# Strided V copies moved to VectorE, one w_out sum moved to GpSimd, and a piece list of its own for chunk 1

## The chip, the cores and the metric

The kernel runs on one core of a Trainium2 chip. The time is the device time of one execution in microseconds (us); several executions of each kernel are measured and their median is taken. A profiled execution gives the trace: what each engine did, when, and what ended its waits. The engines are TensorE (PE, with its weight loads PEld), VectorE (DVE), ScalarE (ACT), GpSimd (POOL) and SyncE (SP, which here only issues DMAs). Each engine works through its own queue in order.

## The reference

```python
def _attn_ref(q, k, v):                      # 8 batches, 8 heads, 576 positions, 64 wide
    ...
    mask_local = (rel >= 0) & (rel < stride)                  # heads 0 to 3, stride 32
    mask_strided = (rel >= 0) & (pos[None, :] % stride == pos[:, None] % stride)   # heads 4 to 7
    ...
    scores = np.where(masks[None, :, :, :], scores, -1000000000.0)
    ...
    return np.matmul(attn, v).astype(np.float32)

def _moe_ref(x, w_in, w_out, alpha):         # 4608 tokens, 512 -> 2048 -> 512
    h = x @ w_in
    g = np.maximum(h, 0.0) + alpha * np.minimum(h, 0.0)
    return (g @ w_out).astype(np.float32)
```

The attention's output, with the heads side by side, is the `x` of the two-layer network. Half of the heads look at the 32 latest positions, the other half at positions that are equal modulo 32.

## The kernel before

**Attention.** Two heads make a pair, four pairs a batch: two local ones, then two strided ones. Pairs are numbered g = 0 to 31, so batch 2 is pairs 8 to 11. The work on a pair is cut into pieces that are put into one list: T and Tk transpose q and k of two pairs (`transpose_piece`); S computes the scores, their exponentials on ACT and a multiplication by the mask on GpSimd (`score_both`, masks on lines 421 and 428); P multiplies with V and divides by the row sums on DVE (`pv_piece`, reciprocal on line 456, multiplication on line 458); X transposes the result into `xT` (`x_piece`), which for most pairs a DMA transposition does in its place. S hands the second half of its exponentials and its mask to a list `defer`, from which each later step takes one entry. PSUM for P, T, X and half of S comes from one pool of three buffers (`ps`).

The strided heads' V is loaded into `stv` (`load_v`, line 169) and copied, 72 partitions by 1024 elements for each half, into `vs`, where each head row has a column of ones beside it (`cast_v`, through `cast_copy`, line 189 on GpSimd and 187 on DVE).

**Network.** The tokens are worked in nine chunks of 512, over a ring `xT` of three batches. Linear 1 has 16 pieces to a chunk (`lin1_piece`): four matmuls into one of three PSUM buffers `hps` (line 627), a ReLU of the negated sum on ACT (line 637), and one DVE instruction that makes `gT` of both (line 639) and frees the buffer. Chunk 0 has a plain linear 2. Chunks 1 to 8 do linear 2 as 2x2 blocks with seven products in place of eight, each product in two pieces of eight matmuls (`fast_piece`, line 696). This needs sums of blocks of `gT` (`g_sums`: four sums, each in a LOW and a HIGH half of 128x1024 elements, written to `sg`) and sums of blocks of `w_out`, made once (`w_sums`: three written to `wt`, the fourth written over a block of `wout16`). All of them are DVE instructions on line 645. Product P6 needs sum 1, P5 sum 0, P7 sum 2, P3 sum 3.

**Order.** It is written out by hand and kept. While chunk n runs (30 pieces: 16 of linear 1, then 14 of linear 2), the attention of batch n+1 is put between its pieces. `acc` spreads the attention pieces evenly, at a lower rate (0.4) in linear 1; chunk 1 has 22 of them, as the list starts up there, the next chunks 17. The sums of `gT` come after the pieces that `SUMS` names. In chunk 1 the two halves of the fourth `w_out` sum come after pieces 2 and 5. Copies, loads and casts of the next batch hang on attention pieces: `cast_v` of batch c on the P pieces of step g = 4c (for batch 2 on the S piece of step 8), the load of the next strided V behind the second copy.

In the list, 22 pieces stand in chunk 1: Tq, Tk for pairs 8 and 9; S8; S9, two P of pair 8; S10, two P of pair 9; S11, P, Tq, P, Tk, P (pair 10, and q and k for pairs 12 and 13); S12 and three P of pair 11; S13, one P of pair 12, X of pair 11. The last one ends the `xT` that chunk 2 needs.

Of the kernel before, what the change touches and what calls it, by code (L numbers as in the profile page):

```python
# [10 lines left out]
F16 = mybir.dt.float16  # L11
ALU = mybir.AluOpType
# [19 lines left out]
def kernel(  # L32
# [10 lines left out]
    nc = tc.nc  # L43
# [7 lines left out]
    FAST = 1  # L51

    LOW, HIGH = slice(0, 4), slice(4, 8)
    SUMS = {10: [(0, LOW)], 16: [(1, LOW)], 17: [(0, HIGH)], 18: [(1, HIGH)],
            20: [(2, LOW)], 21: [(2, HIGH)], 23: [(3, LOW)], 25: [(3, HIGH)]}

# [2 lines left out]
    cpool = ctx.enter_context(tc.tile_pool(name="const", bufs=1))  # L59
    spool = ctx.enter_context(tc.tile_pool(name="stage", bufs=3))  # L60
    tpool = ctx.enter_context(tc.tile_pool(name="tl", bufs=4))
    hpool = ctx.enter_context(tc.tile_pool(name="half", bufs=4))
# [12 lines left out]
            name=nc.get_next_instruction_name(), act_func_set_id=6, ins=[], outs=[]  # L75
# [9 lines left out]

    win16 = cpool.tile([128, 4, 2048], F16)
    wout16 = cpool.tile([128, 16, 512], F16)
    wt = cpool.tile([128, 3, 8, 256], F16)
    xT = cpool.tile([128, 4, RING], F16)

    NE = 6
# [14 lines left out]
    def load_qk(b, strided, nm):  # L106

        h0 = 4 if strided else 0  # L110
        src = q if nm == "q" else k
        if strided and b:
            t16 = hpool.tile([128, 2, 512], F16, tag=f"{nm}s", bufs=3, name=f"{nm}s")
            cast16[(b, True, nm)] = t16
        else:
            t16 = hpool.tile([128, 2, 512], F32, tag=f"{nm}l", bufs=2, name=f"{nm}l")
            loaded[(b, strided, nm)] = t16
        base = src[b, h0 : h0 + 1, 0:1, :]
        eng = nc.sync if (b > 2 and not strided) or (b == 0 and strided) else nc.gpsimd
        keep(eng.dma_start(t16, bass.AP(  # L120
            tensor=base.tensor, offset=base.offset,
            ap=[[8 * D, 64], [2 * S * D, 2], [S * D, 2], [1, 8 * D]])))
# [11 lines left out]
            keep(nc.sync.dma_start_transpose(o, qks[nm].rearrange("p h c -> p (h c)")))  # L134

    def cast_s(b, nm, eng):
        t16 = hpool.tile([128, 2, 512], F16, tag=f"{nm}s", bufs=3, name=f"{nm}s")
        if eng[0] == eng[1]:
            cast_copy(eng[0], t16, loaded[(b, True, nm)])
        else:  # L140
            for f in range(2):
                cast_copy(eng[f], t16[:, f : f + 1, :], loaded[(b, True, nm)][:, f : f + 1, :])
        cast16[(b, True, nm)] = t16
# [47 lines left out]
    def cast_v(b, pr, eng):  # L191

        v16 = vss[b % 2]
        cast_copy(eng, v16[0:72, 2 * pr : 2 * pr + 2, :, 0:64],
                  loaded[b][0:72, 1024 * pr : 1024 * pr + 1024].rearrange(
                      "p (h t d) -> p h t d", h=2, t=8))
        cast16[(b, True, "v")] = v16
# [294 lines left out]
    npair = 4 * B  # L492
# [44 lines left out]
    for g in range(7, npair + 2):  # L537
        c = g // 4
        a, p, t = g, g - 1, g + 1
        okA = 8 <= a < npair  # L540
        okP = 8 <= p < npair
        okT = 8 <= t < npair and (t % 4 == 0 or t < 4 * DX and t % 2 == 0)
        nP = len(pairs[p].pgroups) if okP else 0
        seq = []
        if okA:
            seq.append(("S", lambda a=a: score_both(pairs[a])))
        if okP:
            seq.append(("P", Pv(p, 0)))
        if okT:
            seq.append(("T", T(t // 2, "q")))  # L550
        if 8 <= g - 2 < npair and not pairs[g - 2].xd:
            seq.append(("X", X(g - 2)))
        if okP:
            seq.append(("P", Pv(p, 1)))
        if okT:
            seq.append(("Tk", T(t // 2, "k")))
        if nP == 3:
            seq.append(("P", Pv(p, 2)))
        if not seq:
            seq.append(("N", lambda: None))  # L560

        todo = [(c, pr) for pr in range(2)] if g % 4 == 0 and 8 <= g < npair else []

        if g % 4 == 1 and 9 <= g and c + 1 < B:
            todo = [(c + 1, nm) for nm in "qk"]
        lastP = max([i for i, z in enumerate(seq) if z[0] == "P"], default=len(seq) - 1)
        nslots = [i for i, z in enumerate(seq) if z[0][0] != "S"] or list(range(len(seq)))
        for i, (kind, fn) in enumerate(seq):
            extra = []
            if todo and i in nslots:  # L570
                left = len([z for z in nslots if z >= i])
                cnt = -(-len(todo) // max(1, left))
                extra = [todo.pop(0) for _ in range(min(cnt, len(todo)))]

            def run(fn=fn, extra=extra, g=g, c=c, kind=kind, lastp=(i == lastP), first=(i == 0)):
                fn()
                for b, pr in extra:
                    if pr in ("q", "k"):
                        cast_l(b, pr, "act")
                        if b + 1 < B:  # L580
                            load_qk(b + 1, False, pr)
                        continue
                    cast_v(b, pr, "pool")
                    if pr == 1 and b + 1 < B:
                        load_v(b + 1, True)
                if kind == "Tk" and g % 4 == 3 and c + 3 < B:
                    load_tail(c + 3, False)
                if lastp:
                    if 4 * DX <= g - 1 < npair and pairs[g - 1].xd:
                        x_dma(pairs[g - 1])  # L590
                    if g % 4 == 3 and DX <= c + 1 < B:
                        transpose_d()
                    if g % 4 == 2 and DX <= c and c + 1 < B:
                        load_d(c + 1)
                    if g % 4 == 1 and DX < c and c + 1 < B:
                        load_v(c + 1, False)
                if first and 4 * DX <= g - 3 < npair and pairs[g - 3].xd and pairs[g - 3].strided:
                    x_copy(pairs[g - 3])
            feed(run, g - 2 if kind == "X" else -1)
# [39 lines left out]
        keep(nc.vector.scalar_tensor_tensor(  # L639
            gTs[n][:, m, :], neg, oma[:, m : m + 1], hps, op0=ALU.mult, op1=ALU.add))  # L640

    sums = {}

    def sub(eng, o, x, y, op=ALU.subtract):
        keep(eng.tensor_tensor(o, x, y, op=op))  # L645

    def g_sums(n, k, P):

        if k == 0 and P.start == 0:
            sums["t"] = cpool.tile([128, 4, 8, 256], F16, tag="sg", name="sg")  # L650
        st, g = sums["t"], gTs[n].rearrange("r (p j) t -> r j p t", j=2)
        lo, hi = slice(0, 256), slice(256, 512)
        x, y, op = (
            (g[:, 0, P, hi], g[:, 1, P, hi], ALU.add),
            (st[:, 0, P], g[:, 0, P, lo], ALU.subtract),
            (g[:, 0, P, lo], g[:, 0, P, hi], ALU.subtract),
            (g[:, 1, P, lo], st[:, 1, P], ALU.subtract))[k]
        sub(nc.vector, st[:, k, P], x, y, op)

    def w_sums(k, P):  # L660

        w = wout16.rearrange("r (p j) c -> r j p c", j=2)
        lo, hi = slice(0, 256), slice(256, 512)
        o, x, y, op = (
            (wt[:, 0, P], w[:, 1, P, hi], w[:, 0, P, hi], ALU.subtract),
            (wt[:, 1, P], wt[:, 0, P], w[:, 0, P, lo], ALU.add),
            (wt[:, 2, P], w[:, 1, P, lo], wt[:, 1, P], ALU.subtract),
            (w[:, 0, P, hi], w[:, 0, P, hi], w[:, 0, P, lo], ALU.subtract))[k]
        sub(nc.vector, o, x, y, op)

    PRODUCTS = ("P1", "P4", "P2", "P6", "P5", "P7", "P3")
    cur = {}
# [1 line left out]
    def fast_piece(n, i):  # L674

        name, tb = PRODUCTS[i // 2], i % 2
        last = n == NCH - 1
        g = gTs[n].rearrange("r (p j) t -> r j p t", j=2)
        w = wout16.rearrange("r (p j) c -> r j p c", j=2)
        st = sums["t"]  # L680
# [3 lines left out]
            "P4": ("Z", g[:, 1, :, hi], wt[:, 2]),  # L684
            "P2": ("X", g[:, 1, :, lo], w[:, 1, :, lo]),
            "P6": ("Y", st[:, 1], wt[:, 1]),
            "P5": ("Z", st[:, 0], w[:, 0, :, hi]),
            "P7": ("Y", st[:, 2], wt[:, 0]),
            "P3": ("V", st[:, 3], w[:, 1, :, hi]),
        }[name]  # L690
# [3 lines left out]
        z = cur[bank]  # L694
# [159 lines left out]
    def attn_n(n, end):  # L854
        for _ in range(n):
            attn_step(end)
        if n == 0:
            attn_step(0)
# [30 lines left out]
    for n in range(1, NCH):  # L889
        ab = attn_until(n + 1) if n + 1 < B else len(pieces)  # L890
        left = ab - pos["i"]
        acc = 0.0
        for i in range(30):
            if i < 16:
                lin1_piece(n, i)
                if n == 1 and i in (2, 5):
                    w_sums(3, slice(0, 4) if i == 2 else slice(4, 8))
            else:
                fast_piece(n, i - 16)
            for which, part in SUMS.get(i, ()):  # L900
                g_sums(n, which, part)
            acc += left / (18.4 if n == B - 2 else 19.6) * (0.4 if i < 16 else 1.0)
            cnt = int(acc)
            acc -= cnt
            attn_n(cnt, ab)
        while pos["i"] < ab:
            attn_step(ab)
# [30 lines left out]
```

## Time and profile before

| | us |
|---|---|
| median of three runs | 320.64 |
| lowest, highest | 318.5, 324.51 |
| profiled execution | 317.97 |
| its span, first to last instruction | 316.0 |

| engine | busy us | share of the span |
|---|---|---|
| TensorE | 302.8 | 96% |
| VectorE | 244.2 | 77% |
| ScalarE | 193.0 | 61% |
| GpSimd | 139.0 | 44% |

Linear 1 (line 627) holds 134.2 us of TensorE's busy time. The longest groups on DVE are line 639 (104.5 us, 144 instructions of 743 ns) and the sums of `gT` (60 us in three forms). GpSimd's are the masks (24 on each of two lines, 1.29 and 1.33 us each) and 14 copies of strided V (1.2 us each).

A line of the timeline reads: start, length (both us), engine, line of the program, operation, output<-input, partitions and elements, and in brackets the idle time before it and what ended it. A busy TensorE is not TensorE at its peak: its matmuls overlap, and their ends are modelled.

### The profile page before, as it was taken

To read this page: it belongs to the slowest core of one execution; us is meant where nothing else is said; L and a number is where in the kernel's file an instruction comes from. 1 tells how busy PE (TensorE), PEld (TensorE's weight loads), DVE (VectorE), ACT (ScalarE), POOL (GpSimd) and SP (SyncE) were. 2 spreads that over 40 slices of the span, in tenths; PEclk is the share of its full clock that TensorE was granted. 3 is DMA by queue.
4 is the path that set the end of the run, shared out by engine and by line. 5 is a ranking of instruction groups with operands and counts; after the bars stand their busy time and mean duration, and the time that the engine had idled before them with its cause. 6 is when DMAs were issued, how large, how long until landed. Compare 5 with 4: busy or idle time off the path is not lost.

```text
span 316.0 us, 7306 instructions
## 1 busy us (share of the span) xinstructions
PE 302.8 (96%) x2925; PEld 202.5 (64%) x2925; DVE 244.2 (77%) x436; ACT 193.0 (61%) x353; POOL 139.0 (44%) x144
## 2 busy tenths in 40 slices
PE   8999989998799999999999999999999999999994
PEld 3564455553478448877984488448866884685483
DVE  6476878569997699779977997799778978937862
ACT  2755655389366866686668666866667446525620
POOL 8772399509287444844484438443813300000000
PEclk9999999999799999999999999999999999999999
DMA  7999999999179993799279919971730140003012
GB/s 239 181 207 207 218 212 182 177 246 226 21 91 202 232 129 34 139 263 147 34 139 231 180 25 141 184 95 23 147 111 3 22 119 33 2 33 103 0 35 100
DMA packets 81553, 40.39 MB, mean 128 GB/s; under 512 B 58464, under 2 KB 77168, under 8 KB 81520
## 3 DMA queue, kind: packets, MB, share of 16 engines
q0 software_dynamic: 41728, 17.38, 45.7%
q1 hardware_dynamic: 39792, 22.55, 29.7%
q8 instruction: 23, 0.38, 0.5%
q14 instruction: 10, 0.08, 0.1%
HBM read 38.01 MB, written 9.44 MB: 150 GB/s over the span
## 4 chain that ended last, share of the span: by engine, by line
PE 78%; DVE 9%; ACT 8%; issue 2%; DMA 2%; SPq 1%; ACTq 0%
PE hps L627 35%; PE fZ L696 8%; PE fY L696 8%; PE fX L696 8%; PE ops L762 4%; PE pv L449 4%; DVE sg L645 4%; DVE gT L639 2%; PE fV L696 2%; PE tp L245 2%; DMA alpha_r<-in_moe_alpha_dram 2%; ACT xT L488 2%; PE wps L784 2%; PE sp L406 2%; ACT neg L637 1%
## 5 line engine op out<-in xcount | busy, mean ns | idle before, releaser
L627 PE MATMUL hps<-xT,win 128*128 128x512 f16 (+2 forms) x704 | 134.2, 342 | 5.1 <-DVE gT L639 3.6
L639 DVE SCALAR_TENSOR_TENSOR gT<-neg,oma,hps 128x512 f16<-128x512 f32 x144 | 104.5, 743 | 29.3 <-ACT neg L637 22.4
L637 ACT ACTIVATE neg<-hps 128x512 f32<-128x512 f32 x144 | 85.6, 599 | 44.5 <-PE hps L627 44.5
L627 PEld LDWEIGHTS <-win 128*128 128x128 f16 x704 | 63.6, 98 | 61.6 <-issue 8.3
L421 POOL TENSOR_TENSOR et<-et,consts 128x576 f16<-128x576 f16 (+1 forms) x24 | 31.0, 1290 | 91.2 <-ACT et L419 91.1
L696 PEld LDWEIGHTS <-sg 128*128 128x128 f16 x512 | 47.0, 98 | 5.8
L696 PEld LDWEIGHTS <-gT 128*128 128x128 f16 x384 | 35.9, 98 | 5.5
L458 DVE TENSOR_TENSOR x<-pv,rc 96x384 f16<-96x384 f32 (+2 forms) x62 | 33.0, 532 | 2.1
L696 PE MATMUL fY<-wt,sg 128*128 128x256 f16 x256 | 32.4, 273 | 0.0
L696 PE MATMUL fX<-wout,gT 128*128 128x256 f16 x256 | 32.0, 274 | 0.0
L428 POOL TENSOR_TENSOR et<-et,consts 128x576 f16<-128x576 f16 (+1 forms) x24 | 31.8, 1326 | 0.2 <-ACT et L425 0.2
L449 PEld LDWEIGHTS <-et 72*128 72x128 f16 (+1 forms) x448 | 24.1, 98 | 8.2 <-DVE x16s L458 0.6
L645 DVE TENSOR_TENSOR sg<-gT 128x1024 f16<-128x1024 f16 x32 | 26.7, 852 | 0.0
L456 DVE RECIPROCAL rc<-pv 72x6 f32<-72x6 f32 (+2 forms) x80 | 14.7, 183 | 14.2 <-PE pv L449 14.0
L419 ACT ACTIVATE et<-sp 128x576 f16<-128x576 f32 (+1 forms) x24 | 15.5, 645 | 8.2 <-PE sp L406 7.5
L425 ACT ACTIVATE et<-sph 128x288 f16<-128x288 f32 (+1 forms) x48 | 18.7, 407 | 0.0
L784 PE MATMUL wps<-wrm 128*128 128x512 f16 x44 | 16.4, 449 | 1.2 <-DVE wrm L796 1.2
L645 DVE TENSOR_TENSOR sg<-sg,gT 128x1024 f16<-128x1024 f16 x16 | 16.8, 1048 | 0.2
L189 POOL COPY vs<-stv 72x1024 f16<-72x1024 f16 x14 | 16.7, 1200 | 0.0
L696 PE MATMUL fZ<-wt,gT 128*128 128x256 f16 x128 | 16.3, 272 | 0.0
L762 PE MATMUL ops<-wout,gT 128*128 128x512 f16 x64 | 16.3, 379 | 0.0
L696 PE MATMUL fZ<-wout,sg 128*128 128x256 f16 x128 | 16.3, 272 | 0.0
(110 smaller groups left out, 340.4 us busy)
## 6 DMA issues: line engine op xcount, KB each, us to landing
out_dram<-o SPq DMA_DIRECT2D x24, 256.0 KB, 2.5
ql<-in_q_dram SPq DMA_DIRECT2D x6, 512.0 KB, 6.0
kl<-in_k_dram SPq DMA_DIRECT2D x6, 512.0 KB, 6.8
stv<-in_v_dram POOLq DMA_DIRECT2D x8, 288.0 KB, 6.9
vl<-in_v_dram POOLq DMA_DIRECT2D x6, 384.0 KB, 9.7
win<-in_moe_w_in_dram POOLq DMA_DIRECT2D x4, 512.0 KB, 10.5
wout<-in_moe_w_out_dram POOLq DMA_DIRECT2D x4, 512.0 KB, 13.8
out_dram<-oc SPq DMA_DIRECT2D x8, 256.0 KB, 3.4
```

Of the source, the lines that this page charges most:

```text
L421: keep(nc.gpsimd.tensor_tensor(mv, mv, m, op=ALU.mult))
L425: keep(nc.scalar.activation(ev[:, n * y : n * y + n], sps[y][0:r, 0:n], AF.Exp, scale=SCALE))
L428: keep(nc.gpsimd.tensor_tensor(mv, mv, m, op=ALU.mult))
L449: keep(nc.tensor.matmul(pv[:, 65 * x : 65 * x + 65], et[0:r, c : c + 128], v16[0:r, 2 * P.pr + hh, t, :] if P.strided else v16[:, 6 * (2 * ...
L458: keep(nc.vector.tensor_tensor(P.x16[0:w, c0 : c0 + 64 * nb].rearrange("r (c e) -> r c e", e=64), pvv[:, :, 0:64], rc[0:w, 0:nb].unsqueeze ...
L627: keep(nc.tensor.matmul(hps[:, dst : dst + w], win16[:, kk, 128 * m : 128 * m + 128], xT[:, kk, src : src + w], start=(kk == 0 and x == 0) ...
L637: keep(nc.scalar.activation(neg, hps, AF.Relu, scale=-1.0))
L639: keep(nc.vector.scalar_tensor_tensor(gTs[n][:, m, :], neg, oma[:, m : m + 1], hps, op0=ALU.mult, op1=ALU.add))
L645: keep(eng.tensor_tensor(o, x, y, op=op))
L696: keep(nc.tensor.matmul(z[:, 256 * tb : 256 * tb + 256], x[:, p, 128 * tb : 128 * tb + 128], y[:, p], start=(opens and p == 0 and tb == 0) ...
L762: keep(nc.tensor.matmul(ops, gTs[n][:, kf, 128 * mt : 128 * mt + 128], wout16[:, kf, :], start=(kf == 0), stop=(kf == 15)))
L784: keep(nc.tensor.matmul(wps, wrm[:, 0:128], wrm, start=True, stop=True))
```

## The change

Six edits. (1) The strided V copies of batches 2 to 7 are made by DVE instead of GpSimd; those of batch 2 stand behind linear-1 pieces 1 and 2 of chunk 1 instead of in the scores of pair 8, and the load of batch 3's strided V moves with them. (2) The fourth `w_out` sum is written to a fourth place in `wt`, by GpSimd, and stands behind pieces 0 and 1 instead of 2 and 5; product P5 reads it there. (3) In chunk 1 the number of attention pieces behind each piece is read from `PACE1`. (4) The sums of `gT` in chunk 1 are placed by `SUM1` (n: ahead of the attention pieces of piece n, n.5: behind them; entry z is sum z // 2, HIGH where z is odd). (5) `sg` is one tile for the whole kernel. (6) The pools of the first strided q and k have two buffers instead of three.

```diff
+    SUM1 = {8.5: [0], 18.5: [2], 19.0: [1, 3, 5], 20.5: [4], 22.0: [7], 24.5: [6]}
+    PACE1 = (0, 1, 0, 0, 1, 0, 1, 0, 0, 0, 1, 1, 0, 1, 0, 1, 1, 1, 1, 2, 1, 1, 2, 0, 1, 2, 0, 1, 1, 1)
...
-    wt = cpool.tile([128, 3, 8, 256], F16)
+    wt = cpool.tile([128, 4, 8, 256], F16)
...
-        todo = [(c, pr) for pr in range(2)] if g % 4 == 0 and 8 <= g < npair else []
+        todo = [(c, pr) for pr in range(2)] if g % 4 == 0 and 8 < g < npair else []
...
-                    cast_v(b, pr, "pool")
+                    cast_v(b, pr, "dve")
                     if pr == 1 and b + 1 < B:
                         load_v(b + 1, True)
...
-    sums = {}
+    sums = {"t": cpool.tile([128, 4, 8, 256], F16, name="sg")}
...
-        if k == 0 and P.start == 0:
-            sums["t"] = cpool.tile([128, 4, 8, 256], F16, tag="sg", name="sg")
...
-            (w[:, 0, P, hi], w[:, 0, P, hi], w[:, 0, P, lo], ALU.subtract))[k]
-        sub(nc.vector, o, x, y, op)
+            (wt[:, 3, P], w[:, 0, P, hi], w[:, 0, P, lo], ALU.subtract))[k]
+        sub(nc.gpsimd if k == 3 else nc.vector, o, x, y, op)
...
-            "P5": ("Z", st[:, 0], w[:, 0, :, hi]),
+            "P5": ("Z", st[:, 0], wt[:, 3]),
...
         for i in range(30):
             if i < 16:
                 lin1_piece(n, i)
-                if n == 1 and i in (2, 5):
-                    w_sums(3, slice(0, 4) if i == 2 else slice(4, 8))
+                if n == 1 and i in (1, 2):
+                    cast_v(2, i - 1, "dve")
+                    if i == 2:
+                        load_v(3, True)
+                if n == 1 and i in (0, 1):
+                    w_sums(3, slice(4 * i, 4 * i + 4))
             else:
                 fast_piece(n, i - 16)
+            if n == 1:
+                for z in SUM1.get(i, ()):
+                    g_sums(n, z // 2, HIGH if z % 2 else LOW)
+                attn_n(PACE1[i], ab)
+                for z in SUM1.get(i + 0.5, ()):
+                    g_sums(n, z // 2, HIGH if z % 2 else LOW)
+                continue
             for which, part in SUMS.get(i, ()):
                 g_sums(n, which, part)
             acc += left / (18.4 if n == B - 2 else 19.6) * (0.4 if i < 16 else 1.0)
```

Before, the 22 pieces of chunk 1 stood behind pieces 2, 4, 6, 8, 11, 13 and 15 of linear 1 and about one behind each piece of linear 2. With `PACE1`, the first T stands behind piece 1 and the scores of pair 9 behind piece 10; the number in linear 1 is seven in both.

More of the change, by code (lines that the diff above doesn't have):

```diff
@@ L112, in load_qk @@
         if strided and b:
-            t16 = hpool.tile([128, 2, 512], F16, tag=f"{nm}s", bufs=3, name=f"{nm}s")
+            t16 = hpool.tile([128, 2, 512], F16, tag=f"{nm}s", bufs=2, name=f"{nm}s")
             cast16[(b, True, nm)] = t16
@@ L136, in cast_s @@
     def cast_s(b, nm, eng):
-        t16 = hpool.tile([128, 2, 512], F16, tag=f"{nm}s", bufs=3, name=f"{nm}s")
+        t16 = hpool.tile([128, 2, 512], F16, tag=f"{nm}s", bufs=2, name=f"{nm}s")
         if eng[0] == eng[1]:
```

## The prediction

> **What bounds the kernel now.** I read the summary page first, then busy time by stretches, then the chain of waits and the timeline where a stretch stood out.
>
> The page: engine totals, and of the 40 slices the TensorE row and its granted clock.
>
> ```profile
> PE 302.8 (96%) x2925; PEld 202.5 (64%) x2925; DVE 244.2 (77%) x436; ACT 193.0 (61%) x353; POOL 139.0 (44%) x144
> ...
> PE   8999989998799999999999999999999999999994
> ...
> PEclk9999999999799999999999999999999999999999
> ```
>
> TensorE (PE) is busy nearly everywhere. One slice, the eleventh (79.0 to 86.9 us), has both less work and a lower clock. So a change in what VectorE (DVE) and GpSimd (POOL) do can only pay near there.
>
> The stretches (us, PE busy, weight loads, DVE, ACT, POOL, clock, DMA share, GB/s): chunk 1 in four, the stall alone, the slow clock alone, and a stretch of chunk 2 for comparison.
>
> ```profile
> 62.80:77.50 14.70, 14.70 (x112) 7.40 (x111) 10.72 (x15) 13.01 (x26) 6.25 (x7) 1.00 1.34 240
> 77.50:84.30 6.80, 3.48 (x28) 1.30 (x24) 6.37 (x9) 2.52 (x5) 1.86 (x2) 0.79 0.22 36
> 84.30:102.10 17.80, 17.01 (x226) 14.17 (x221) 15.26 (x29) 11.03 (x23) 14.46 (x13) 0.98 0.84 127
> 102.10:104.00 1.90, 1.12 (x12) 0.60 (x12) 0.66 (x1) 1.90 (x5) 1.84 (x3) 1.00 0.89 199
> 77.40:80.60 3.20, 0.21 (x7) 0.12 (x4) 3.20 (x3) 1.60 (x3) 1.96 (x2) 1.00 0.50 82
> 81.50:84.90 3.40, 3.10 (x24) 1.30 (x23) 2.79 (x6) 1.61 (x3) 0.00 (x0) 0.50 0.11 19
> ```
>
> ```profile
> 119.00:135.00 16.00, 16.00 (x206) 14.09 (x205) 13.60 (x26) 10.89 (x21) 10.95 (x11) 1.00 0.54 84
> ```
>
> Chunk 1 runs from 62.8 to about 104, 41 us; chunk 2 from 104 to 135.5, 31.5, with PE full. Up to 77.5 chunk 1 is full too. Then PE stands for 3.2 us, and while it restarts its granted clock is 0.50 for 3.4 us.
>
> The timeline shows what it stood for:
>
> ```profile
> 75.62 1.30 POOL L428 TENSOR_TENSOR et<-et,consts 128x576 f16<-128x576 f16 x1
> 75.98 3.94 DVE L645 TENSOR_TENSOR sg<-gT 128x1024 f16<-128x1024 f16 x1
> ...
> 76.86 1.28 POOL L421 TENSOR_TENSOR et<-et,consts 128x576 f16<-128x576 f16 x1
> ...
> 78.09 1.27 POOL L428 TENSOR_TENSOR et<-et,consts 128x576 f16<-128x576 f16 x1
> 79.84 0.73 DVE L639 SCALAR_TENSOR_TENSOR gT<-neg,oma,hps 128x512 f16<-128x512 f32 x1
> ...
> 80.63 1.05 PE L627 MATMUL hps<-xT,win 128*128 128x512 f16 x4 [3.02 <-DVE gT L639]
> ```
>
> The first sum of chunk 1 takes 3.94 us where the median of its group is 0.68. It ends 0.56 after the third of three GpSimd masks that follow each other without a gap. Behind it on DVE wait the L639 results that free the three hps buffers; PE waits for those. So two DVE inputs in SBUF and a running GpSimd operation exclude each other here. In chunk 2 the same collision is shorter: a sum at 130.03 takes 1.79, ending 0.55 after the one mask in its way, and PE does not notice.
>
> **What the stall costs.** From 77.5 to 84.3, 6.8 us, PE does two linear-1 pieces (8 matmuls of 0.219, 1.75) and one score piece (about 0.45). 6.8 - 2.2 = 4.6 us are lost, standing time and slow clock together. In 84.3 to 102.1 PE is idle for 0.8, and 0.6 us still run at half clock, 0.3. So 4.6 + 0.8 + 0.3 = 5.7, with the 0.7 before the next chunk 6.4, is the most that chunk 1 can give back.
>
> **The change, part by part.**
>
> *First sum moved, scores of pair 9 two pieces later.* The sum now stands behind piece 8 instead of 10. PE reaches the end of piece 8 at 62.8 + 9 x 0.875 + transposes 1.5 + scores 0.45 = 72.6; ReLU 0.6 and L639 0.75 follow, so the sum is due at about 74.0. Pair 8's two masks, no longer parted by two GpSimd copies (2.0) and a DMA issue (0.8), run about 71.5 to 74.1; pair 9's come only after piece 10, from about 75.7. The sum falls into the gap: 0.7 to 0.8. Bounds: 0.68 and the 3.94 of today. If it meets one mask, it costs 1.3 more; DVE has 11.7 (16 x 0.73) + 0.9 + 0.7 + 1.5 = 14.8 us of work between 64.8 and about 81, so 81 - 64.8 - 14.8 = 1.4 is covered. Then the stall goes, with the slow clock: -4.6. Next in line is ACT, which ends its cast of kl at 79.0 in the present trace; the last two ReLUs would end at 80.2, in time for the first fast piece at about 80.0, which needs them only after 0.7.
>
> *Batch 2's V copies to DVE, behind pieces 1 and 2, and the last w_out sum to GpSimd.* DVE loses two sums of 0.68 and gains two copies; the nearest rows are the DVE copies of batch 0:
>
> ```profile
> L187 DVE COPY vs<-stv x2: 425/520/614, 12.2 to 12.5; 72x1024 f16<-72x1024 f16 x2
> ```
>
> so 2 x 0.52 against 1.36: even. GpSimd's sum has no row. Below it lies a copy of 1024 elements with one input, 1.03; above, a two-input mask of 576 elements at 1.27, by length 2.26. I take 2.26, since it has two inputs. Behind the vl load, which ends at 61.85, two of them fill GpSimd to 66.4; the first copy is due on DVE at 66.3. Cost 0 to 0.5, covered. What queues behind them on GpSimd: the strided V load of batch 3 (0.81, now earlier than its 74.80) and the tails' two loads (1.3), needed some 20 us later. SyncE's order is unchanged. The sum's place of its own removes only a write after read; the fast product needs it at about 91.
>
> One thing can spoil this. In front of GpSimd's first two-input operation stand two of these:
>
> ```profile
> L421 POOLq MODIFY_POOL_CONFIG  x2: 62/62/62, 63.1 to 63.1; - x2
> ```
>
> The next GpSimd operation starts at 71.52, released by ACT; whatever the reconfiguration takes is hidden in 8.4 us of idling. Now the sums follow it at once. The bound is 0 to 8.4 us; I take 0 for the forecast, as the rows show 62 ns, and give the rest to a rival.
>
> [...]
>
> *The rest of the sums in chunk 1.* (1, LOW) comes two pieces later than now, and three more follow it in one block behind piece 19, among masks of pairs 10 and 11. Four sums cost 2.7 alone; each may meet one mask (the rows show 1.06 to 1.76 for such sums today). I find pair 10's first result at about 89.0, and PE, which wants its PSUM buffer for the k transposes at 87.5, may wait up to 1.5. Today's order loses 0.8 there. Between 0 and 1.5 I take 1.1, which cancels the 0.8 and the 0.3 of clock: net 0, range -1.1 to +0.4.
>
> *V copies of batches 3 to 7.* In each of five chunks GpSimd loses 2 x 1.03, DVE gains 2 x 0.52. In chunk 2 the first is due at 129.04, just when mask one ends (127.77 + 1.27) and the exponential of mask two is ready: if the copy goes first, mask two runs to 130.8, the second copy ends at 131.2 and the sum at 131.9, against 131.81 today, because that sum no longer waits for 1.1. Behind it, the result that PE transposes at 134.27 is finished at 132.36 now: 1.9 us of cover. Cost 0, with cover gone the rival below.
>
> **The sum.** -4.6 + 0 + 0 + 0. Profiled execution: 317.97 (span 316.0 and 1.97 around it), so 313.4. The median of the runs, 320.64, is 2.67 above that one; on it I put 320.64 - 4.6 = **316.0 us**.
>
> **Rivals.**
>
> *The reconfiguration takes time (25%).* At half the bound, 4.2 us, the sums run from 66.1 to 70.6; the first copy, due at 66.3, waits for one or both, to 68.4 or 70.6, and L639 queues behind it: 2.1 to 4.3, less the 1.4 that DVE catches up with before PE needs its buffers. At the full 8.4 the copies are free, but the sums and the loads behind them end at 76.9, pair 8's first mask at 78.2, and PE, which wants it at 75.1, stands for 3.1. Either way about 2.5 of the gain is gone: 318.5 (317.5 to 320). For it: nothing in the trace limits it but the 8.4. Against: the first mask, at 1.35, is hardly longer than the others.
>
> *Everything is regained (20%).* The block of sums finds its gaps; all 6.4 come back: 314.2. Against: four sums in a row have not been free of masks anywhere before 104.
>
> *The copies on DVE hold up every chunk (12%).* If mask two always starts before the copy, each copy waits a mask: 2 x 1.7 = 3.4, less the 1.1 that today's sum waits. Above the 1.9 of cover it costs 0.4 a chunk; with no handover between masks, as at 75.98, another 1.3 at least. Five times 1.3 is 6.5, minus 4.6: 322.5, slower than before; five times 2.2 gives 327. It decides from 0.9 us a chunk. Against: most collisions in the trace end after one mask.
>
> **Chances and range.** The forecast has 43%, its own range 313.5 to 318. Over 2% (below 314.2 or above 327.1) is about what a measurement of this kernel can tell from no change, its three runs lying between 318.5 and 324.51. Faster by more: half of "everything" and the lower end of the forecast, with the spread of the median, 0.27. Slower by more: the far end of the copies, 0.06. Within: 0.67. The range reaches from 312 (everything, and a quick set of runs) to 322.5.
>
> **What would show it.** Right: no sum in chunk 1 over 2 us, no slice with a lower clock near 80, chunk 2's first matmul near 99.5 instead of 104, the distance between chunks 2 and 3 still 31.5. Wrong: a gap between the reconfiguration and the first GpSimd sum; copies of V on DVE over 1.5 us with PE waiting behind them; a new wait of the k transposes for pair 10.

## The result

| | before | after |
|---|---|---|
| median of 20 runs, us | 321.14 | 319.98 |
| ratio after / before | | 0.9927, 95% interval 0.9899 to 0.9954 |
| first ReLU of chunk 1 to first ReLU of chunk 2, us (first, second profile) | 40.60, 40.58 | 38.16, 37.65 |
| of it linear 1 (to the first matmul of linear 2) | 20.25, 20.25 | 16.64, 15.92 |
| of it linear 2 | 20.34, 20.33 | 21.52, 21.73 |
| the same distance for chunk 2 | 31.53, 31.54 | 31.54, 31.54 |

Both kernels have some slower executions among the 20: the ratio is of the fast ones alone, the medians are of all. By the ratio the kernel became faster by 0.7%, some 2.3 us; the forecast was 4.6. The whole gain lies in chunk 1, and it is made of two parts of opposite sign: linear 1 gives 3.6 to 4.3 us, linear 2 takes 1.2 to 1.4 back.

In the first profiled execution of after, TensorE's granted clock was 0.51 from 11 to 21 us, and chunk 1 begins 7.2 us later than in the profile of before; whole spans (320.5 and 316.0) are therefore not compared, distances within the execution are. Those repeat well: the distances of chunks 2 to 7 agree within 0.03 us in all kernels below, and two profiles of before agree in chunk 1 within 0.02.

The page of after, engine totals, TensorE by slices and its clock:

```profile
PE 304.7 (95%) x2925; PEld 203.5 (63%) x2925; DVE 240.1 (75%) x446; ACT 193.1 (60%) x353; POOL 127.6 (40%) x134
...
PE   6799998999888899999999999999999999999995
...
PEclk9669999999999999999999999999999999999999
```

The low clock in the eleventh slice is gone; the one near the start belongs to this execution. GpSimd has 11 us less to do. PE's dip in slice 11 is the end of chunk 1's linear 1, those in slices 12 to 14 are its linear 2.

The same stretches of both kernels, from the first ReLU of chunk 1 to the first matmul of linear 2, from there to chunk 2, and chunk 2. Columns: window, its length, then busy time of PE, PEld, DVE, ACT and POOL, granted clock, DMA share, GB/s. First before:

```profile
64.12:84.37 20.25, 16.93 (x130) 8.11 (x129) 17.04 (x22) 15.01 (x28) 7.83 (x7) 0.93 0.94 179
84.37:104.72 20.35, 18.78 (x239) 15.10 (x236) 15.91 (x29) 13.58 (x27) 17.02 (x15) 0.99 0.85 133
104.72:136.25 31.53, 31.45 (x323) 21.68 (x321) 26.36 (x47) 22.64 (x42) 17.69 (x18) 1.00 0.87 133
```

and after, first profile:

```profile
71.30:87.94 16.64, 15.74 (x130) 7.75 (x129) 13.37 (x23) 15.06 (x29) 9.21 (x8) 1.00 1.43 180
87.94:109.46 21.52, 18.61 (x240) 15.17 (x236) 16.43 (x31) 13.66 (x25) 13.51 (x13) 1.00 0.91 148
109.46:141.00 31.54, 31.46 (x323) 21.71 (x321) 26.23 (x49) 22.67 (x42) 16.06 (x16) 1.00 0.90 148
```

In linear 1 the standing time fell from 3.3 to 0.9 us, and the clock is back at 1.00. In linear 2 PE's work is the same and its idle time rose from 1.6 to 2.9. Chunk 2 is the same to a hundredth, although two copies changed engines in it.

The timeline of after around the first sum, which lasted 3.94 us before:

```profile
79.95 1.27 POOL L430 TENSOR_TENSOR et<-et,consts 128x576 f16<-128x576 f16 x1
...
80.97 0.80 DVE L647 TENSOR_TENSOR sg<-gT 128x1024 f16<-128x1024 f16 x1
...
82.62 1.27 POOL L423 TENSOR_TENSOR et<-et,consts 128x576 f16<-128x576 f16 x1 [1.40 <-ACT et L421]
```

The sum now starts in the last quarter of a microsecond of pair 8's second mask, pair 9's first comes 1.4 us behind that one, and the sum takes 0.80. And the new wait, in linear 2:

```profile
91.89 0.74 POOL L129 DMA_DIRECT2D ksd<-in_k_dram  x1
...
92.33 3.38 DVE L647 TENSOR_TENSOR sg<-sg,gT 128x1024 f16<-128x1024 f16 x1
...
92.62 1.31 POOL L423 TENSOR_TENSOR et<-et,consts 72x576 f16<-72x576 f16 x1
...
93.86 1.29 POOL L430 TENSOR_TENSOR et<-et,consts 72x576 f16<-72x576 f16 x1
...
95.64 0.68 DVE L647 TENSOR_TENSOR sg<-gT 128x1024 f16<-128x1024 f16 x1
...
96.45 0.55 DVE L460 TENSOR_TENSOR x16s<-pv,rc 72x384 f16<-72x384 f32 x1
...
97.06 0.62 PE L247 MATMUL tp<-consts,kl 128*128 128x128 f16 x8 [2.05 <-DVE x16s L460]
```

(1, HIGH), the third of the four sums in the block, starts 0.3 us ahead of pair 11's first mask, loses to it and to the second, and ends 0.56 after that. (2, HIGH) and pair 10's first result stand behind it on DVE. That result holds a PSUM buffer of `ps`, and the k transposes wait 2.05 us for the buffer.

### The profile page after: what moved, and what is told of

Its sections match the earlier page's. It is cut to its first block, busy times and chain, and to the rows that moved or that the text cites. A ratio compares the mean times of both kernels' runs of the same rounds, so it can differ in the third digit from the quotient of the medians.

```text
span 320.5 us, 7312 instructions
## 1 busy us (share of the span) xinstructions
PE 304.7 (95%) x2925; PEld 203.5 (63%) x2925; DVE 240.1 (75%) x446; ACT 193.1 (60%) x353; POOL 127.6 (40%) x134
## 4 chain that ended last, share of the span: by engine, by line
PE 78%; DVE 7%; ACT 6%; DMA 6%; issue 2%; SPq 0%; ACTq 0%
PE hps L629 33%; PE fX L696 8%; PE fZ L696 8%; PE fY L696 8%; DMA kT<-ksd 4%; PE pv L451 4%; PE ops L762 3%; PE wps L784 2%; DMA kl<-in_k_dram 2%; PE fV L696 2%; DVE sg L647 2%; PE tp L247 2%; ACT xT L490 2%; PE sp L408 2%; DVE gT L641 2%
## 5 line engine op out<-in xcount | busy, mean ns | idle before, releaser
L639 ACT ACTIVATE neg<-hps 128x512 f32<-128x512 f32 x144 | 85.7, 600 | 40.4 <-PE hps L629 40.1
L423 POOL TENSOR_TENSOR et<-et,consts 128x576 f16<-128x576 f16 (+1 forms) x24 | 30.6, 1274 | 93.7 <-ACT et L421 93.7
L430 POOL TENSOR_TENSOR et<-et,consts 128x576 f16<-128x576 f16 (+1 forms) x24 | 31.2, 1302 | 5.5 <-ACT et L427 4.7
L647 DVE TENSOR_TENSOR sg<-gT 128x1024 f16<-128x1024 f16 x32 | 21.8, 696 | 0.0
L784 PE MATMUL wps<-wrm 128*128 128x512 f16 x44 | 17.8, 478 | 1.2 <-DVE wrm L796 1.2
L647 DVE TENSOR_TENSOR sg<-sg,gT 128x1024 f16<-128x1024 f16 x16 | 18.5, 1157 | 0.3
L696 PE MATMUL fZ<-wt,sg 128*128 128x256 f16 x128 | 16.3, 272 | 0.0
L696 PE MATMUL fV<-wout,sg 128*128 128x256 f16 x128 | 16.1, 273 | 0.0
```

The costliest lines, as they stand in the source:

```text
L423: keep(nc.gpsimd.tensor_tensor(mv, mv, m, op=ALU.mult))
L430: keep(nc.gpsimd.tensor_tensor(mv, mv, m, op=ALU.mult))
L639: keep(nc.scalar.activation(neg, hps, AF.Relu, scale=-1.0))
L696: keep(nc.tensor.matmul(z[:, 256 * tb : 256 * tb + 256], x[:, p, 128 * tb : 128 * tb + 128], y[:, p], start=(opens and p == 0 and tb == 0) ...
L784: keep(nc.tensor.matmul(wps, wrm[:, 0:128], wrm, start=True, stop=True))
```

## The experiments

All times of chunk 1 below are from its first ReLU to chunk 2's first.

**The changed kernel again** (no edit).

> The changed kernel, unaltered, for a second profile. Theory: the change acts in chunk 1 alone, so the distance from chunk 1's first ReLU (line 639) to chunk 2's is again near 38.2 us (before: 40.6), and chunks 2 to 8 keep their distances (31.5, 31.6, 31.5, 31.0, 29.7, 26.4) within 0.1. The wait of pair 10's scores for the k transposition (1.1 us) depends on DMA traffic and may differ by some tenths; the wait of the k transposes in linear 2 (2.3 us) comes back, since nothing but engine order makes it. Rival: the first profile's late start (its first matmuls ran at half clock) shaped chunk 1; then the distance differs from 38.2 by more than 0.5.

Measured: chunk 1 37.65; the six later distances as expected. The k transposes waited 2.26 us, so the new wait belongs to the order. Chunk 1 lies 0.55 from 38.2, just past the bound of the rival: a part of the first profile is its own. Linear 1 is 0.7 shorter and linear 2 is 0.2 longer. In linear 1 the wait for the DMA transposition of k (PE 0.65 in the first profile, landing 12.0 us after issue) shrank to 0.4 on the weight loads alone, with a landing of 10.9. The new stretches:

```profile
67.04:82.96 15.92, 15.68 (x131) 7.76 (x129) 12.64 (x22) 14.70 (x28) 9.19 (x8) 1.00 1.43 198
82.96:104.69 21.73, 18.61 (x240) 15.15 (x236) 17.35 (x32) 13.88 (x27) 13.47 (x13) 1.00 0.93 139
```

**Before again** (no edit).

> Before, unaltered, for a second profile. In the first, (1, HIGH) started 0.27 us ahead of a mask and ran free (0.68 us); in the run with the moved w_out sum alone it started 0.28 ahead of the same mask and took 3.35 us, and linear 2 of chunk 1 took 21.7 instead of 20.3. Theory A (the edit shifted it over an edge): here it runs free again, linear 2 of chunk 1 20.3 to 20.4, chunk 1 40.4 to 40.8. Rival B (a race that goes either way in one and the same kernel): 3.3 us and 21.7.

Measured: linear 1 20.25, linear 2 20.33, chunk 1 40.58; (1, HIGH) 0.68, started 0.27 ahead of a mask. Theory A: the two profiles of this kernel repeat it (0.68 both times), and with the w_out sum moved it took 3.35.

**The list alone**: before with `PACE1` and `SUM1`.

```diff
+    SUM1 = {8.5: [0], 18.5: [2], 19.0: [1, 3, 5], 20.5: [4], 22.0: [7], 24.5: [6]}
+    PACE1 = (0, 1, 0, 0, 1, 0, 1, ...
+            if n == 1:
+                for z in SUM1.get(i, ()):
+                    g_sums(n, z // 2, HIGH if z % 2 else LOW)
+                attn_n(PACE1[i], ab)
...
+                continue
```

> Before, with the piece list and the sums of chunk 1 alone; V copies and the w_out sum as before, so that two V copies and a load stand on GpSimd between pair 8's masks again. Theory A (the list removes the stall by taking pair 9's masks away from the first sum): the first sum is under 2 us, no slow clock near 80, chunk 1 near 38.2 to 39, ratio about 0.993. Rival B (the copies on GpSimd are what pushes the second mask into the sum): the second mask of pair 8 still starts near 75.6, past the sum at 74, so the sum is free, but pair 8's second P waits; or the sum meets copies and lasts 2 to 3 us; chunk 1 stays at 39.5 to 40.6, ratio 0.997 to 1.0.

Measured: chunk 1 37.77 (linear 1 16.08, linear 2 21.70), ratio 0.9943 (0.9877 to 1.0009). The first sum met two copies on GpSimd and took 1.59, which VectorE caught up with; (1, HIGH) took 3.32, and the k transposes waited 2.2. That is after's chunk 1 without the moved copies and sum, so the list alone makes gain and loss. Edits (5) and (6) are not in this kernel either, and chunk 1 takes the same without them.

**The V copies alone**.

```diff
-                    cast_v(b, pr, "pool")
+                    cast_v(b, pr, "dve")
```

> Before, with the strided V copies of batches 2 to 7 on VectorE and nothing else. Theory A: steady chunks keep 31.5 to 31.6 us (the copies lie in cover); in chunk 1 pair 8's second mask moves forward by about 2.8 us, but pair 9's two masks still meet the first sum, so the sum lasts 2 to 3 us instead of 3.9 and chunk 1 takes 39 to 40; ratio 0.995 to 1.0. Rival B: without the copies the masks end before the sum starts and this alone gives all of the change's gain: chunk 1 near 38.2, ratio 0.993. Rival C: copies delay each chunk: distances of chunks 2 to 5 grow by 0.3 or more.

Measured: chunk 1 43.74, 3.1 us longer than before; ratio 1.0222 (1.0154 to 1.0290). None of the three: steady chunks keep 31.5 (31.53, 31.61, 31.52), but batch 2's two copies, at their old place in pair 8's scores, now do what the sum did. Timeline of this kernel:

```profile
75.64 1.35 POOL L421 TENSOR_TENSOR et<-et,consts 128x576 f16<-128x576 f16 x1 [8.44 <-ACT et L419]
...
76.44 5.37 DVE L187 COPY vs<-stv 72x1024 f16<-72x1024 f16 x2
76.95 0.81 POOL L169 DMA_DIRECT2D stv<-in_v_dram  x1
77.77 1.30 POOL L428 TENSOR_TENSOR et<-et,consts 128x576 f16<-128x576 f16 x1
79.01 1.28 POOL L421 TENSOR_TENSOR et<-et,consts 128x576 f16<-128x576 f16 x1
80.24 1.27 POOL L428 TENSOR_TENSOR et<-et,consts 128x576 f16<-128x576 f16 x1
81.73 0.73 DVE L639 SCALAR_TENSOR_TENSOR gT<-neg,oma,hps 128x512 f16<-128x512 f32 x1
```

The first copy waits for one mask, the second for three, and L639 stands behind them. The first sum, later for that, then runs free. In linear 1 this costs 1.7 of the 3.1 us (21.96). The other 1.4 come in linear 2 (21.78), where (1, HIGH) takes 3.36 under pair 11's two masks; in before it took 0.68 there. In after, the same copies stand behind pieces 1 and 2, where GpSimd has no mask, and take 0.42 each.

**The w_out sum alone**: before with the fourth sum on GpSimd behind pieces 0 and 1, in a place of its own, and with the smaller pools of edit (6).

```diff
-            (w[:, 0, P, hi], w[:, 0, P, hi], w[:, 0, P, lo], ALU.subtract))[k]
-        sub(nc.vector, o, x, y, op)
+            (wt[:, 3, P], w[:, 0, P, hi], w[:, 0, P, lo], ALU.subtract))[k]
+        sub(nc.gpsimd if k == 3 else nc.vector, o, x, y, op)
...
-                if n == 1 and i in (2, 5):
-                    w_sums(3, slice(0, 4) if i == 2 else slice(4, 8))
+                if n == 1 and i in (0, 1):
+                    w_sums(3, slice(4 * i, 4 * i + 4))
```

> Before, with the fourth w_out sum on GpSimd behind pieces 0 and 1, in a place of its own, and nothing else. Theory A: GpSimd takes about 2.1 us for each half, begins at once after the reconfiguration, is done before the first mask; VectorE has 1.4 us less to do, but the first sum of chunk 1 still meets the three masks: chunk 1 40.2 to 40.6, ratio 0.999 to 1.0. Rival B: VectorE, earlier by up to 1.4 us, meets the sum with the masks in another place and the stall changes by more than 1 us either way.

Measured: chunk 1 41.93, ratio 1.0074 (1.0022 to 1.0127): rival B's size, in another place than either theory said. Linear 1 did not change (20.23; the first sum 3.83). Linear 2 went from 20.34 to 21.70, because (1, HIGH), which ran free 0.27 us ahead of a mask, now starts 0.28 ahead of it and takes 3.35. Why so small a shift turns it is not shown.

**The sums' places alone**: `SUM1` with the old pace.

> Before, with the places of chunk 1's sums alone (the attention pieces keep their old pace). Theory A (what counts is that the first sum starts before pair 9's masks are queued): it meets at most the V copies on GpSimd, lasts under 2.3 us, chunk 1 loses most of its stall: 37.5 to 38.5. Rival B (the scores of pair 9 at their old place, behind piece 8, still put three GpSimd operations in its way): 3 us or more, chunk 1 39.5 to 41.

Measured: 43.45 (linear 1 22.13, linear 2 21.32, where (1, HIGH) takes 3.33). Rival B, and worse: the first sum waits for the second of two copies and then, through a DMA issue of 0.8 us, for three masks:

```profile
81.54 6.12 DVE L646 TENSOR_TENSOR sg<-gT 128x1024 f16<-128x1024 f16 x1
82.54 0.81 POOL L170 DMA_DIRECT2D stv<-in_v_dram  x1
83.36 1.30 POOL L429 TENSOR_TENSOR et<-et,consts 128x576 f16<-128x576 f16 x1
84.59 1.28 POOL L422 TENSOR_TENSOR et<-et,consts 128x576 f16<-128x576 f16 x1
85.83 1.27 POOL L429 TENSOR_TENSOR et<-et,consts 128x576 f16<-128x576 f16 x1
```

**The pace alone**: `PACE1` with the old places of the sums.

> Before, with the pace of chunk 1's attention pieces alone (the sums keep their old places, the first behind piece 10). Theory A: the first sum starts near 76, while pair 8's second mask runs (75.6 to 76.9) and pair 9's are two pieces later, so it waits for one mask or, if not let in between, for three: 1.3 to 3.9 us; chunk 1 38 to 40.6. Rival B (the pace alone is the gain): the sum is free and chunk 1 is at 37.7 or below.

Measured: 40.11, theory A near its slow end: the first sum 4.25, under three masks. Neither half of the list removes the stall; the sum has to come earlier and pair 9's masks later.

**The load of batch 3's strided V later**: after, with it behind piece 11.

> After, with the load of batch 3's strided V behind piece 11 instead of 2. In after's first profile pair 10's scores waited 1.1 us for the k transposition by DMA (12.0 us from issue to landing); in the second profile they did not. Theory A (that wait came from the late start of that execution, not from the load): chunk 1 as in the second profile, 37.6 to 37.7. Rival B (the earlier load competes with the transposition): chunk 1 shorter than 37.65 by 0.2 or more, or the landing of the transposition under 8 us.

Measured: chunk 1 37.63, that of the second profile, and no wait for the transposition: theory A by this bound. But the transposition landed 7.0 us after issue, which is rival B's other bound. DMA issues, with the time to landing, in the first profile of after:

```profile
kT<-ksd SPq DMA_TRANSPOSE x1, 12.0
```

and in this kernel:

```profile
kT<-ksd SPq DMA_TRANSPOSE x1, 7.0
```

The four profiles with the load behind piece 2 show 10.8 to 12.0 for it, the eight with the load at its old place 6.2 to 6.8. So the earlier load makes the transposition land 4 to 5 us later. PE waited for that 0.65 us in the first profile of after and 0.3 with the block taken apart (below), and not at all in the other two; why one execution of after shows 12.0 and the other 10.9 stays open.

**Pair 11's masks left out**: after, without the two multiplications.

```diff
-                keep(nc.gpsimd.tensor_tensor(mv, mv, m, op=ALU.mult))
+                if P.g != 11:
+                    keep(nc.gpsimd.tensor_tensor(mv, mv, m, op=ALU.mult))
...
-                if y:
+                if y and P.g != 11:
```

> After, with the two mask multiplications of pair 11 on GpSimd left out (batch 2's last two strided heads are then not masked). Theory A (the two masks make (1, HIGH) last 3.35 us, and that makes the wait of the k transposes): the sum lasts 0.7, the wait is gone or under 0.3, linear 2 of chunk 1 takes 19.3 to 19.7 us instead of 21.6. Rival B (four sums in a row hold pair 10's results whatever GpSimd does): the sum is short, but the k transposes still wait 0.5 or more and linear 2 takes 20.3 or more.

Measured: (1, HIGH) 0.69, no wait of the k transposes, linear 2 19.96, chunk 1 35.88. The masks are the cause. Linear 2 stays 0.3 over the expected range: X of pair 11 waits 0.8 us for an exponential there, where the other kernels show 0.3 or less. Timeline, the four sums in a row and the transposes without a wait:

```profile
85.67 0.97 DVE L648 TENSOR_TENSOR sg<-sg,gT 128x1024 f16<-128x1024 f16 x1
...
86.57 0.68 DVE L648 TENSOR_TENSOR sg<-gT 128x1024 f16<-128x1024 f16 x1
...
87.28 0.69 DVE L648 TENSOR_TENSOR sg<-sg,gT 128x1024 f16<-128x1024 f16 x1
...
87.89 0.69 DVE L648 TENSOR_TENSOR sg<-gT 128x1024 f16<-128x1024 f16 x1
...
89.56 0.61 PE L247 MATMUL tp<-consts,kl 128*128 128x128 f16 x8
```

**The block taken apart**: after with two of its sums behind pair 10's results.

```diff
-    SUM1 = {8.5: [0], 18.5: [2], 19.0: [1, 3, 5], 20.5: [4], 22.0: [7], 24.5: [6]}
+    SUM1 = {8.5: [0], 18.5: [2], 19.0: [1], 20.5: [3, 4], 22.0: [5], 23.0: [7], 24.5: [6]}
```

> After, with the block of sums in chunk 1 taken apart: (1, HIGH) and (2, LOW) come behind pair 10's second P, (2, HIGH) and (3, HIGH) behind the two transposes. Theory A (the 3.35 us of (1, HIGH) under two masks holds pair 10's two results, these hold a PSUM buffer, and the k transposes wait 2.05 to 2.3 us for it): pair 10's masks find the queue of VectorE without a waiting sum, the wait of the k transposes falls under 0.5, chunk 1 goes from 37.65 (the second profile of after) to 35.5 to 36.2; ratio to before 0.984 to 0.989, better than after's 0.9927. Rival B: the sums only meet the next masks (pair 11's) and the wait moves to products P6 or P7, which need them; chunk 1 stays at 37 or above and the ratio at 0.992 to 0.996.

Measured: chunk 1 35.64, linear 2 19.34, the k transposes without a wait; ratio 0.9903 (0.9838 to 0.9968). Theory A in the profile; the ratio of whole runs does not separate it from after's.

```profile
90.38 0.55 DVE L460 TENSOR_TENSOR x16s<-pv,rc 72x384 f16<-72x384 f32 x1
...
91.34 1.29 POOL L430 TENSOR_TENSOR et<-et,consts 72x576 f16<-72x576 f16 x1
...
91.89 0.55 DVE L460 TENSOR_TENSOR x16s<-pv,rc 72x384 f16<-72x384 f32 x1
92.34 0.61 PE L247 MATMUL tp<-consts,kl 128*128 128x128 f16 x8
92.36 0.83 DVE L647 TENSOR_TENSOR sg<-sg,gT 128x1024 f16<-128x1024 f16 x1
```

Pair 10's two results, which have one input in PSUM and one in SBUF, take 0.55 us under the masks as they do elsewhere; (1, HIGH) comes when the second mask is nearly done.

**List and spread sums alone**: before with `PACE1` and that `SUM1`, copies and w_out sum where they were.

> Before, with the piece list of chunk 1 and the sums taken apart as in the spread experiment; V copies on GpSimd and the w_out sum on VectorE as before. Theory A (the list and the sums' places are all of the gain, the move of the copies and of the w_out sum adds nothing): chunk 1 35.4 to 36.0, as in spread (35.64), ratio 0.984 to 0.991. Rival B (the moved copies and the moved sum make the room that the spread sums need): chunk 1 36.5 or more, with a sum over 2 us.

Measured: chunk 1 35.42 (16.08 and 19.34), ratio 0.9818 (0.9748 to 0.9888). Theory A. By chunk 1 and by the ratio it is the best version of the study, and its interval lies below after's. It has none of the moved copies, not the moved sum and not the earlier load. The 5.2 us of chunk 1 alone would make, as an estimate, a ratio of 0.984 on before's 321, which lies in the interval.

```profile
66.85:82.93 16.08, 15.84 (x130) 7.79 (x129) 13.81 (x22) 14.70 (x28) 7.84 (x7) 1.00 1.15 224
82.93:102.27 19.34, 18.49 (x240) 15.13 (x236) 14.66 (x30) 13.80 (x27) 16.25 (x15) 1.00 0.81 114
```

## Why the prediction was half right

The direction, the place and the cause of the gain were right; the size was twice what came, because a cost in linear 2 was put too low. That the time lies in the range says little, as before's own 321.14 lies in it too. By the prediction's own terms:

- *The stall in linear 1, -4.6.* It went, with its slow clock. Measured -3.6 and -4.3 in the two profiles. What is missing is a short wait for the k transposition (0.65 us of PE in the first profile, gone in the second) and 0.2 for L639. The prediction named ACT as next in line; it was these two. The first of them comes of the change itself: the load of batch 3's strided V, moved ahead of the transposition, was counted only with its 0.81 us on GpSimd, and the transposition landed 12.0 and 10.9 us after its issue instead of 6.2.
- *The rest of the sums in chunk 1, net 0 with a range of -1.1 to +0.4.* This is the step that failed. It named the wait, the k transposes behind pair 10's results, and allowed it 1.1 us; it lasted 2.05 and 2.26, and linear 2 became longer by 1.2 and 1.4. The mis-sized part is the cost of a sum among masks: at most one mask for each was counted, since most collisions in the trace ended after one (1.62 to 1.79 us for the eight sums of chunks 2 to 5 that began during a mask), though the first sum of before had waited for three (3.94). (1, HIGH) waited for two (3.38 and 3.35). With the masks left out, or the sums put elsewhere, the wait is gone, so this cause is shown.
- *V copies of batch 2 and the w_out sum, even.* In after they cost nothing: the list alone gives the same chunk 1 (37.77 against 37.65). By themselves both did harm: the copies 1.7 us at their old place and 1.4 through (1, HIGH), the sum 1.3 through (1, HIGH). The prediction weighed each of them only inside the whole change.
- *V copies of batches 3 to 7, 0.* Right: five chunks unchanged within 0.03 us. In chunk 2 the first copy took 0.41 and let mask two wait (1.34), the second 0.77, and the sum behind them ended 26.69 us after the chunk's first ReLU, 27.09 before; 0.1 later had been expected.
- *The reconfiguration of GpSimd, taken as 0, rival 25%.* It cost nothing: the issue of the vl load ends at 69.03, and the sums begin at 69.12, 0.09 us later against the rival's 4.2 to 8.4. They take 4.22 together, 2.11 each, near the 2.26 taken by length. The two reconfigurations, 0.04 us each, lie between.

```profile
67.59 1.44 POOL L179 DMA_DIRECT2D vl<-in_v_dram  x1 [10.69 <-PE pv L451]
...
69.12 4.22 POOL L647 TENSOR_TENSOR wt<-wout 128x1024 f16<-128x1024 f16 x2
```

```profile
L647 POOLq MODIFY_POOL_CONFIG  x2: 38/40/42, 69.0 to 69.1; - x2
```

Of the rivals, "everything is regained" named what the spread sums then did: 5.0 and 5.2 us in chunk 1 against its 6.4. "The copies hold up every chunk" did not happen in any chunk from 2 on.

## What to carry to other kernels

When a stall is taken out by reordering, the operations that made it are still there: lay every moved VectorE operation of the kinds that lasted longer here (the sums, with both inputs in SBUF: 0.68 us alone, up to 6.12 beside GpSimd's operations; the V copies, from SBUF to SBUF: 0.42 alone, 5.37 for two) beside the GpSimd operations near its new place, and see whose PSUM buffer stands behind it. The sums of before's chunks 2 to 5 that began during a mask ended after that one (1.62 to 1.79), but allow for the whole unbroken run of them, above all where a DMA issue of GpSimd stands directly ahead of it (3.94 and 4.25 under three masks, 6.12 with a copy ahead of them). A load that is moved ahead of another DMA can delay that one's landing (7.0 us became 10.8 to 12.0 here), so look up who waits for it too. Where a change bundles an order with moved work, try the order by itself first, and compare distances between marks inside one execution when the start varies by more than the effect.

## What the runs showed of the hardware that was not expected

A VectorE operation that started ahead of a GpSimd mask did not always end ahead of it. Sums that began 0.24 to 0.29 us ahead of a mask waited for both masks that followed (3.32 to 3.38 us, in seven profiles), and a copy that began 0.57 ahead waited for three (4.61 of the 5.37 above). All eight began while GpSimd was issuing a DMA. That alone does not decide it: (1, HIGH), 0.27 ahead of the mask and likewise begun during a DMA issue, ran free in both profiles of before (0.68) and with the pace alone. In before:

```profile
88.76 0.71 POOL L127 DMA_DIRECT2D ksd<-in_k_dram  x1
...
89.20 0.68 DVE L645 TENSOR_TENSOR sg<-sg,gT 128x1024 f16<-128x1024 f16 x1
...
89.48 1.54 POOL L421 TENSOR_TENSOR et<-et,consts 72x576 f16<-72x576 f16 x1
```

Where GpSimd was issuing no DMA, all 25 sums in the thirteen profiles that began up to 0.58 us ahead of a GpSimd operation took 0.68 to 0.69. One that began 0.56 ahead (247.59 in before) left the mask at 1.27; one that began 0.19 ahead made it 1.63, with the list and the spread sums alone:

```profile
92.57 0.68 DVE L647 TENSOR_TENSOR sg<-gT,sg 128x1024 f16<-128x1024 f16 x1
...
92.76 1.63 POOL L423 TENSOR_TENSOR et<-et,consts 128x576 f16<-128x576 f16 x1 [1.18 <-ACT et L421]
```

Of the operations that began during a mask most got in at its end (1.62 to 1.79 for those eight of before): at 85.18 in before a sum took 1.73, between two masks that touch, and the second of these took 1.72 instead of 1.27. But others waited for all three, one that began 0.06 us into the first of them (4.25, with the pace alone) and one 0.37 into it (3.94); in both a DMA issue of GpSimd had ended directly ahead of that first mask. What decides it stays open; none of the edits was made to test it.
